# Later loads of x, early products of ones and a shifted zero fill in a chunked attention and mixture-of-experts kernel

## The chip, the cores and the metric

The kernel runs on one core of one Trainium2 chip. The metric is the device time of one execution in microseconds. "TensorE" (PE in the profile) multiplies matrices, "VectorE" (DVE) and "ScalarE" (ACT) work on elements, "GpSimd" (POOL) issues indirect transfers, and "SyncE" (SP) issues most of the other transfers.

## The reference

Chunked attention is followed by a mixture of experts, of which each token takes one. All is float32.

```python
B, H, S, D = 4, 8, 768, 64            # batch, heads, sequence, width of a head
chunk, left_ctx, right_ctx, n_mem = 32, 16, 8, 8
for c in range(S // chunk):
    k_full = concatenate([mem_k, k[l_start:r_end]])      # 8 memory keys + the chunk with its contexts
    v_full = concatenate([mem_v, v[l_start:r_end]])
    a = softmax(q_c @ k_full.T / sqrt(D))
    out[c] = a @ v_full

x = out.transpose(0, 2, 1, 3).reshape(3072, 512)         # token x (head, width)
logits = x @ w_gate                                      # 8 experts
e = argmax(logits); gate = softmax(logits)[e]
y = gate * (relu(x @ w1[e]) @ w2[e])                     # w1: 8 x 512 x 1024, w2: 8 x 1024 x 512
```

## The kernel before

**Attention.** The work is done in 32 steps of 96 queries (`QB`), step i of them in the loop `for i in range(NB)` (lines 1134 to 1176). Two steps share one load of queries and one load of keys (`load_q`, `load_k`, lines 626 to 636), "superblock" j. SyncE issues these loads, and the loads of v (`load_v`), in program order on its own queue. The buffers hold three superblocks of k and q and six steps of v. The tiles come with the tokens on the partitions, so TensorE turns them (transposes against an identity): `turn_q(m)` and `turn_k(m)` (lines 651 to 680) turn half of a superblock's heads, m = 2j or 2j + 1, into a PSUM bank, and ScalarE or VectorE copy the bank to SBUF. The bank is one of the two of the pool `ps_t`, or one that the caller hands over. `scores(i)` multiplies turned keys and queries (four products of 128 x 128 by 192 columns), and ScalarE takes three exponentials of the result. `values(i, g, bank)` multiplies by v one step later.

Ahead of the loop, superblocks 0 and 1 are turned: `turn_k(0)` and `turn_k(1)` into `ps_t`, `turn_q(0)` and `turn_q(1)` into two banks `first` of the pool `ps_o`, and `turn_k(2)` and `turn_k(3)` into the two halves of one tile `second` of the pool `ps_s`, which `scores` uses too (lines 1125 to 1132). In step i of the loop come, in this order, the loads for three steps ahead, `turn_q(i + 2)`, `scores(i)`, `values(i - 1)`, the turn of finished rows, and `turn_k(i + 4)`. The order of each engine's instructions is that of the program (`manual_schedule`); waits are put in by the framework where tiles depend on each other.

**Routing.** Eight groups of steps get logits, the choice of expert and a row number for each token. The work of a group is queued three steps after its last step and done piece by piece in later steps. Each token's row is then scattered to `x_dram`, a DRAM buffer sorted by expert, by indirect transfers of GpSimd (`scatter_one`, line 847). `behind(i)` (line 841) makes a transfer wait for the TensorE instruction that was issued last. Rows 0 to 255 of `x_dram` are filled with zeros ahead of that: two transfers on GpSimd's queue, written in step 2 (lines 1171 to 1173), which wait for nothing of that step. The rows behind each expert's tokens are filled later (`end_rows`).

**Experts.** From line 1244 on a planner writes the work: `op` (line 1278) notes each step with the semaphore counts it waits for, in program order for each engine, and `emit` writes it. For each expert TensorE has a switch over arms, one for each number of token columns (lines 1840 to 1848): "split" arms do each layer in seven products on sums of blocks (`layer`, line 1545), "plain" arms, for few tokens, do it directly (`plain`, line 1672). A hint for the next expert's arm is put three steps (plain: one) ahead of the arm's end. In a plain arm an engine has fewer steps than in a split one, so its last step raises its semaphore to the count of the split arm (`upto`). In this run experts 1 and 6 are plain. Between two arms `interlude(e)` (line 1639) turns the outputs of expert e - 1 (`turn_y`) and does first sums for expert e.

SyncE's queue in the expert part is what the change is about. In `expert(e)`:

- `load_x(e + 1)` (lines 1402 to 1416) brings the tokens of the next expert in eight transfers of 160 KB, into the one buffer `X`. VectorE empties `X` with two transposes, `turn_x(e + 1, 0)` and `turn_x(e + 1, 1)`, in the second layer of expert e (line 1793), and after them does two weight sums and one token sum `t1[0]` for expert e + 1.
- `get_w(e + 2, 0)` (line 1477) loads w1 of the expert after the next, 2 MB, once ScalarE has come to the middle of expert e.
- `get_w(e + 2, 1)` loads w2 of it, 2 MB, after ScalarE's last output of expert e.

Since the loads of x stand first in `expert(e)`, they come behind w2 of expert e + 1 on the queue, which was issued at the end of expert e - 1.

Of the kernel before, what the change touches and what calls it, by code (L numbers as in the profile page):

```python
# [12 lines left out]
I32 = mybir.dt.int32  # L13
# [13 lines left out]
N, DM, E, F = B * S, H * D, 8, 1024  # L27
# [44 lines left out]
NER = 256  # L72
TAIL = 192
# [454 lines left out]
def ordinary(ctx, tc, q, k, v, mem_k, mem_v, moe_w_gate, moe_w1, moe_w2, out, good):  # L528

    nc = tc.nc  # L530
# [12 lines left out]
    def bc(ap, axis, n):  # L543
        shape = list(ap.shape)
        shape.insert(axis, n)
        idx = tuple([slice(None)] * axis + [None])
        return ap[idx].to_broadcast(shape)
# [339 lines left out]
    def scatter_some(n):  # L887
        while spread and n:
            spread.pop(0)()
            n -= 1  # L890

    def need(i, f, *lists):
        if 0 <= i < NB:
            f(i)
# [219 lines left out]
    with tc.manual_schedule():  # L1114
        load_k(0)
        load_q(0)
        load_k(1)
        load_q(1)
        load_v(0)
        load_k(2)  # L1120
        load_v(1)
        load_q(2)
        load_v(2)

        first = [ps_o.tile([128, 512], F32, tag="o", name="o") for _ in range(2)]
        second = ps_s.tile([128, 2, 512], F32, tag="s", name="sc")
        turn_k(0)
        turn_k(1, nc.scalar.copy)
        turn_q(0, nc.vector.tensor_copy, first[0])
        turn_q(1, bank=first[1])  # L1130
        turn_k(2, bank=second[:, 0])
        turn_k(3, nc.scalar.copy, second[:, 1])
        early_rows()
        for i in range(NB):
            if i // 2 + 3 < NSB:
                (load_k, load_q)[i % 2](i // 2 + 3)
            need(i + 3, load_v)
            need(i + 2, turn_q)
            scores(i)
            scatter_some(1)  # L1140
            banks = [ps_o.tile([128, 512], F32, tag="o", name="o") for _ in range(2)]
            cur["bank"] = banks[0]
            if i <= 23:
                routing(1, "p")
            if i >= 1:
                values(i - 1, 0, banks[0])
            need(i - 2, turn_xb)
            routing(5 if i > 23 else 3)
            done = [g for g in range(len(GROUPS)) if i - 3 == GROUPS[g][1] - 1]
            late = logits(done[0], banks[1]) if done else None  # L1150
            if i >= 1:
                values(i - 1, 1, banks[1])
            if late:
                place_logits(*late)
            if i > 23:
                routing(1, "p")
            scatter_some(1)
            need(i + 4, turn_k)
            routing(6 if i > 23 else 5)
            hold_back()  # L1160
            for g in done:
                work.extend(routed(g))
            if i == 24:
                fetch_w(0, 4)
            if i >= 24:
                fetch_piece(1)
                fetch_piece(1)
            if len(scatters) >= EARLY and "early" not in cur:
                cur["early"] = i
                early_count(banks[0])  # L1170
            if i == 2:
                nc.gpsimd.dma_start(x_dram[0:TAIL].rearrange("(x p) c -> p x c", x=2), bc(zeros.bitcast(I32), 1, 2))
                nc.gpsimd.dma_start(x_dram[TAIL:NER], zeros[0 : NER - TAIL].bitcast(I32))
            if i == 29:
                early_load()
                early_gather()

        do_early(1)
        n = NB

        def bank_pair():
            banks = [ps_o.tile([128, 512], F32, tag="o", name="o") for _ in range(2)]
            cur["bank"] = banks[0]
            return banks

        banks = bank_pair()
        values(n - 1, 0, banks[0])
        scatter_some(1)  # L1190
        turn_xb(n - 2)
        late = last_logits(n - 3, banks[1])
        values(n - 1, 1, banks[1])
        scatter_some(1)
        nc.vector.tensor_copy(*late)
        routing(99, "v")
        fetch_w(1, 1)
        fetch_piece(4)
        do_early(1)
        banks = bank_pair()  # L1200
        late = last_logits(n - 2, banks[1])
        nc.vector.tensor_copy(*late)
        do_early(1)
        turn_xb(n - 1)
        scatter_some(1)
        do_early(1)
        routing(1, "p")
        routing(99, "v")
        hold_back()
        banks = bank_pair()  # L1210
        late = last_logits(n - 1, banks[1])
        nc.vector.tensor_copy(*late)
        fetch_piece(1)
        work.extend(routed(len(GROUPS) - 1))
        routing(99)
        check_sums()
        do_early(2)
        scatter_some(1)
        routing(1, "p")
        routing(99, "v")  # L1220
        hold_back()
        do_early(1)
        scatter_some(1)
        count_up()
        index = []

        def load_index(e):
            index.append(nc.tensor.value_load(cases[0:1, e : e + 1], min_val=0, max_val=len(arms_of(e)) - 1))

        while spread:  # L1230
            scatter_some(1)
            if len(early_ops) == 2:
                load_index(0)
            do_early(1)
        zeroed = end_rows(0)
        for j in scatters:
            tc.declare_no_dep(zeroed.ins, j, reason="rows behind those of the tokens")
        assert len(early_ops) == len(index) == 1
        rv = nc.values_load(good[0:1, 0:1], min_val=0, max_val=1)
        tc.switch_hint({mybir.EngineType.PE: index[0]}, len(arms_of(0)), "expert0")  # L1240
        nc.tensor.addr_align(PAGE, 0, 0)
        do_early(1)
# [514 lines left out]
    def expert(e):  # L1757
        A1, A2 = quarters(e, 0), quarters(e, 1)
        B1 = [[xT[:, 2 * k : 2 * k + 2, 1 - y] for y in range(2)] for k in range(2)]
        b1 = [[x_names(k, y) for y in range(2)] for k in range(2)]  # L1760
        B2 = [[h[:, 4 * k : 4 * k + 4, y] for y in range(2)] for k in range(2)]
        b2 = [[[("h", k, m, y) for m in range(2)] for y in range(2)] for k in range(2)]
        t1n, t2n = [("t1", i) for i in range(3)], [("t2", i % 2) for i in range(3)]
        s1n, s2n = [("s1", i) for i in range(3)], [("s2", i % 2) for i in range(3)]
        s2, (s1, t1) = sums2[e], sums1[e]
        t2 = token_sums(B2, b2, T2, "t2", t2n)
        w1n = [("w1", e % 2, "rest"), ("w1", e % 2, "21")]
        w2n = [("w2", e % 2, "rest"), ("w2", e % 2, "21")]
        if e + 1 < E:
            load_x(e + 1)  # L1770

        def usual():

            for a in range(2):
                hs = [[h[:, 4 * a + 2 * m : 4 * a + 2 * m + 2, y] for y in range(2)] for m in range(2)]
                hn = [[("h", a, m, y) for y in range(2)] for m in range(2)]
                part = [[A1[m][k][:, :, a] for k in range(2)] for m in range(2)]
                at = {
                    0: {5: [t1[2], s1[3]], 6: [t1[3]], 3: [s2[0]]},
                    1: {1: [t2[0]], 6: [s2[1]], 2: [s2[3]]},  # L1780
                }[a]
                layer(e, part, w1n, [x[:, :, a] for x in S1], s1n, B1, b1, T1, t1n, hs, hn, True, a == 1, at)
            assert not sends
            half.append(("ACT", counts["ACT"]))
            if e < E - 1:
                get_x(e + 1)
                tick()
            ys = [[yT[:, 2 * m : 2 * m + 2, 1 - y] for y in range(2)] for m in range(2)]
            yn = [[("y", m, y) for y in range(2)] for m in range(2)]
            at = {1: [t2[1]], 5: [t2[2], s2[2]], 6: [t2[3]]}  # L1790
            if e + 1 < E:
                s1e, t1e = sums1[e + 1]
                at[6].append(lambda: turn_x(e + 1, 0))
                at.update({2: [lambda: turn_x(e + 1, 1)], 7: [s1e[0]], 3: [s1e[1]], 4: [t1e[0]]})
            layer(e, A2, w2n, S2, s2n, B2, b2, T2, t2n, ys, yn, False, True, at)
            assert not sends

        half = []
        either(e, usual, (lambda ends: plain(e, ends)) if can_be_plain(e) else None)
        if e + 2 < E:  # L1800
            get_w(e + 2, 0, half)
        if 0 < e < E - 1:
            op("POOL", one_op(nc.gpsimd.drain))
        if e + 2 < E:
            get_w(e + 2, 1, [("ACT", counts["ACT"])])
# [113 lines left out]
```

## Time and profile before

| | us |
|---|---|
| median of three runs (490.04, 490.1, 492.1) | 490.1 |
| profiled execution | 488.05 |
| its span, first to last instruction | 486.2 |
| TensorE busy | 462.1 |
| VectorE busy | 282.5 |
| ScalarE busy | 207.8 |

A row of a timeline gives the start and the duration in us, the engine, the line, the operation, the tiles (out <- in), their shapes and the number of merged instructions; in brackets stands how long the engine was idle before, and what released it. "SPq" is SyncE's queue, at the time of issue; the transfer comes later. One float32 product shows as two MATMUL records. L534 and L539 are the helpers through which all products and turns go, so the tiles tell them apart: `tqk`, `kn` and `qn` are turns of keys and queries, `sc` scores, `sum_p` to `sum_z` the banks of the experts, `xs` the buffer `X`, `xsT` its transposed form, `yT` the outputs ahead of their turn, and `t` and `s` sums of tokens and weights. DMA queues: q1 is SyncE's, q0 GpSimd's, q8 the one that brings code.

### The profile page before, as it was taken

The page shows a single profiled execution, that of the slowest core. Times are in us where ns is not written, and L with a number is a line of the kernel's source. Part 1 is how long each engine was busy: PE and PEld are TensorE (multiplying, and loading weights), DVE is VectorE, ACT ScalarE, POOL GpSimd, SP SyncE. Part 2 cuts the span into 40 slices and gives each one's busy share as a digit, 9 for nine tenths or more (in the row PEclk, how much of TensorE's full clock was granted, in tenths as well). Part 3 has the DMA queues.
Part 4 walks back from the last instruction along what each step waited for, and adds up shares of the span by engine and source line. Part 5 has one row for each costly group of instructions (what it writes and reads, how often), then busy time and mean ns, then how long its engine had stood idle before and what let it go on. Part 6 is the DMA issues. An engine that isn't in the chain of part 4 may idle for free. (4 is left out here: it accounts for less than half of the span.)

```text
span 486.2 us, 9257 instructions
## 1 busy us (share of the span) xinstructions
PE 462.1 (95%) x3272; PEld 431.4 (89%) x3272; DVE 282.5 (58%) x548; ACT 207.8 (43%) x389; POOL 146.1 (30%) x191
## 2 busy tenths in 40 slices
PE   4999999999999899999999999999999999899992
PEld 3899999999998679899999999977778999889992
DVE  4466676677555668924665867644537784555511
ACT  3676666666632236311452353334214623144312
POOL 3000323323353227334054144022311442442004
PEclk9999999999999999999999999999999999999998
DMA  9999999999989588790997386390714787400002
GB/s 235 176 196 203 207 265 240 239 227 251 283 191 303 154 248 192 158 295 20 222 275 166 102 253 144 67 283 34 152 25 140 241 176 217 124 3 27 1 1 89
DMA packets 103058, 82.98 MB, mean 171 GB/s; under 512 B 40309, under 2 KB 85966, under 8 KB 102992
## 3 DMA queue, kind: packets, MB, share of 16 engines
q1 hardware_dynamic: 94576, 67.94, 59.6%
q0 software_dynamic: 6912, 13.54, 8.4%
q8 instruction: 44, 0.72, 0.7%
q10 hardware_dynamic: 1504, 0.59, 0.5%
q14 instruction: 22, 0.18, 0.1%
HBM read 65.62 MB, written 21.28 MB: 179 GB/s over the span
## 5 line engine op out<-in xcount | busy, mean ns | idle before, releaser
L1446 POOL DMA_INDIRECT out_dram<-y,lab x42 | 50.3, 1198 | 149.0 <-ACT y L1433 30.8
L935 POOL DMA_INDIRECT lab<-x_dram,rows x42 | 51.3, 1222 | 53.9 <-PE sum_q L534 19.6
L534 PE MATMUL o<-v,ex 128*96 128x65 f32 x512 | 52.8, 246 | 0.0
L534 PEld LDWEIGHTS o<-v,ex 128*96 128x96 f32 x512 | 50.4, 165 | 1.4 <-issue 1.3
L534 PE MATMUL sum_p<-xsT,w 128*128 128x144 f32 (+7 forms) x256 | 49.1, 337 | 2.7 <-DVE t L1379 1.7
L534 PE MATMUL sc<-qT,kT 128*128 128x192 f32 x256 | 49.2, 336 | 0.0
L534 PEld LDWEIGHTS sum_p<-xsT,w 128*128 128x128 f32 x256 | 41.8, 190 | 7.0 <-issue 2.6
L534 PE MATMUL sum_p<-h,w 128*128 128x144 f32 (+7 forms) x256 | 46.1, 335 | 0.0
L848 POOL DMA_INDIRECT x_dram<-xr,dest x32 | 29.7, 928 | 52.3 <-PE o L534 34.0
L705 ACT ACTIVATE ex<-sc,cst 128x256 f32<-128x256 f32 x96 | 38.6, 472 | 14.2 <-PE sc L534 12.0
L534 PEld LDWEIGHTS sum_p<-h,w 128*128 128x128 f32 x256 | 41.8, 190 | 2.4
L534 PEld LDWEIGHTS sc<-qT,kT 128*128 128x128 f32 x256 | 42.0, 195 | 0.0
L656 ACT COPY qT<-tqk 64x384 f32<-64x384 f32 x60 | 30.0, 500 | 28.0 <-PE tqk L539 27.2
L1382 ACT COPY sum_r<-sum_p 128x640 f32<-128x640 f32 x36 | 24.4, 677 | 40.9 <-PE sum_p L534 40.6
L674 DVE COPY kT<-tqk 64x384 f32<-64x384 f32 x58 | 32.0, 552 | 11.0 <-PE tqk L539 10.5
L534 PE MATMUL sum_r<-t,w 128*128 128x144 f32 (+5 forms) x192 | 37.0, 340 | 0.0
L534 PE MATMUL sum_p<-t,s 128*128 128x144 f32 (+5 forms) x192 | 36.8, 340 | 0.0
L534 PE MATMUL sum_q<-t,s 128*128 128x144 f32 (+5 forms) x192 | 36.7, 339 | 0.0
L1400 DVE STREAM_TRANSPOSE xsT<-xs 128x1280 f32<-128x1280 f32 (+1 forms) x16 | 22.4, 1426 | 23.9 <-DMA xs<-x_dram 23.9
L534 PEld LDWEIGHTS sum_q<-t,s 128*128 128x128 f32 x192 | 31.9, 190 | 2.3
L534 PEld LDWEIGHTS sum_p<-t,s 128*128 128x128 f32 x192 | 31.9, 190 | 2.4
L534 PEld LDWEIGHTS sum_r<-t,w 128*128 128x128 f32 x192 | 31.8, 190 | 2.3
(183 smaller groups left out, 771.0 us busy)
## 6 DMA issues: line engine op xcount, KB each, us to landing
w<-in_moe_w_dram SPq DMA_DIRECT2D x36, 512.0 KB
w<-in_moe_w_dram SPq DMA_DIRECT2D x7, 2048.0 KB
xs<-x_dram SPq DMA_DIRECT2D x56, 160.0 KB
kn<-in_k_dram SPq DMA_DIRECT2D x16, 384.0 KB
qn<-in_q_dram SPq DMA_DIRECT2D x16, 384.0 KB
x_dram<-zeros SPq DMA_DIRECT2D x8, 396.0 KB
v<-in_v_dram SPq DMA_DIRECT2D x24, 128.0 KB
v<-in_v_dram SPq DMA_DIRECT2D x24, 112.0 KB
```

The lines of the kernel that those rows point to most:

```text
L534: i = nc.tensor.matmul(*args, **more)
L656: copy(to[:, :, :, t], tq[D * t : D * t + D])
L674: i = copy(to, of[:, :, 0:PAIRS].rearrange("d a (y z p) -> d a y z p", y=2, z=2))
L705: nc.scalar.activation(ex4[:, :, :, sl], sc4[:, :, :, sl], AF.Exp, bias=mask[:, 3 * x + g : 3 * x + g + 1], scale=D**-0.5)
L848: i = nc.gpsimd.indirect_dma_start(out=x_dram, out_offset=bass.IndirectOffsetOnAxis(ap=dest[:, t : t + 1], axis=0), in_=xr[:, t % NXR].bit ...
L935: return nc.gpsimd.indirect_dma_start(out=to.bitcast(I32), out_offset=None, in_=x_dram.rearrange("r (k c) -> (r k) c", c=LB), in_offset=ba ...
L1382: op("ACT", one_op(lambda: nc.scalar.copy(to, of)), reads, writes)
L1400: op("DVE", one_op(lambda: nc.vector.transpose(to, of)), [("xs", y, a) for a in range(4)], [("x", k, 1 - y) for k in range(2)])
L1446: return nc.gpsimd.indirect_dma_start(out=out, out_offset=bass.IndirectOffsetOnAxis(ap=which.bitcast(I32), axis=0), in_=y, in_offset=None, ...
```

## The change

There are four edits.

1. Ten products of a 128 x 128 tile of ones with itself, into a bank that is overwritten later, stand ahead of TensorE's first turn.
2. `turn_k(2)` goes to a bank of `ps_t`, and `turn_k(3)` to the first half of `second`: two tiles instead of one. In step 0, `turn_q(2)` stands behind `scores(0)` instead of ahead of it.
3. The zero fill of rows 0 to 255 moves from step 2 to the end of step 5 (the sixth), and waits for TensorE's last instruction there.
4. `load_x(e + 1)` at the start of expert e stays for e = 0 alone. For the others, `load_x(e + 2)` stands in expert e between the loads of w1 and w2 of expert e + 2. It waits for the two transposes that empty `X`.

```diff
         first = [ps_o.tile([128, 512], F32, tag="o", name="o") for _ in range(2)]
         second = ps_s.tile([128, 2, 512], F32, tag="s", name="sc")
+        for _ in range(10):
+            mm(first[0][:, 0:128], lhsT=ones, rhs=ones, start=True, stop=True)
         turn_k(0)
         turn_k(1, nc.scalar.copy)
         turn_q(0, nc.vector.tensor_copy, first[0])
         turn_q(1, bank=first[1])
-        turn_k(2, bank=second[:, 0])
-        turn_k(3, nc.scalar.copy, second[:, 1])
+        turn_k(2)
+        turn_k(3, nc.scalar.copy, second[:, 0])
         early_rows()
         for i in range(NB):
...
             need(i + 3, load_v)
-            need(i + 2, turn_q)
+            if i > 0:
+                need(i + 2, turn_q)
             scores(i)
+            if i == 0:
+                need(i + 2, turn_q)
...
-            if i == 2:
-                nc.gpsimd.dma_start(x_dram[0:TAIL].rearrange("(x p) c -> p x c", x=2), bc(zeros.bitcast(I32), 1, 2))
-                nc.gpsimd.dma_start(x_dram[TAIL:NER], zeros[0 : NER - TAIL].bitcast(I32))
+            if i == 5:
+                behind(
+                    nc.gpsimd.dma_start(
+                        x_dram[0:TAIL].rearrange("(x p) c -> p x c", x=2), bc(zeros.bitcast(I32), 1, 2)
+                    )
+                )
+                behind(nc.gpsimd.dma_start(x_dram[TAIL:NER], zeros[0 : NER - TAIL].bitcast(I32)))
...
-        if e + 1 < E:
-            load_x(e + 1)
+        if e == 0:
+            load_x(1)
...
         either(e, usual, (lambda ends: plain(e, ends)) if can_be_plain(e) else None)
         if e + 2 < E:
             get_w(e + 2, 0, half)
+            load_x(e + 2)
         if 0 < e < E - 1:
             op("POOL", one_op(nc.gpsimd.drain))
```

## The prediction

> **What bounds the kernel now.** First the page: engines, slices, DMA rate.
>
> ```profile
> span 486.2 us, 9257 instructions
> ...
> PE 462.1 (95%) x3272; PEld 431.4 (89%) x3272; DVE 282.5 (58%) x548; ACT 207.8 (43%) x389; POOL 146.1 (30%) x191
> ...
> DMA packets 103058, 82.98 MB, mean 171 GB/s; under 512 B 40309, under 2 KB 85966, under 8 KB 102992
> ```
>
> TensorE is busy for 462.1 of 486.2 us, so a change that adds no speed to its products can win only some of the 24 us that are left. Second, who those 24 us wait for: the waits with TensorE as filter.
>
> ```profile
> PE tqk L539 <- DMA kn<-in_mem_k_dram: 6.0, 1, 6.0
> PE sum_z L539 <- DVE t L1379: 2.0, 1, 2.0
> PE sum_p L534 <- DVE t L1379: 1.7, 1, 1.7
> PE sc L539 <- DVE kT L674: 1.2, 1, 1.2
> PE tqk L539 <- DMA kn<-in_k_dram: 0.7, 2, 0.4
> ```
>
> Three belong to the start (tqk, sc), two to the experts (sum_z, sum_p). Third, the stretches of the start: after TensorE's count come DVE, ACT and POOL, then granted clock, share of the DMA engines and GB/s.
>
> ```profile
> 0.00:15.00 15.00, 7.75 (x36) 6.83 (x36) 5.44 (x12) 5.58 (x11) 4.56 (x21) 1.00 0.99 223
> 15.00:30.00 15.00, 14.34 (x137) 14.15 (x138) 8.48 (x22) 10.64 (x25) 0.00 (x0) 1.00 1.07 181
> 30.00:60.00 30.00, 30.00 (x308) 29.56 (x307) 20.51 (x65) 19.78 (x47) 3.10 (x8) 1.00 1.10 202
> ```
>
> The DMA engines are full (shares about 1) through the first 60 us. TensorE waits for loads until about 23 us, and from 30 us on for nothing: two bounds lie close together. Fourth, the timeline of the start.
>
> ```profile
> 0.84 0.17 DVE L583 MEMSET ones<- 128x128 f32 x1 [0.84 <-PEq L1905]
> ...
> 6.04 1.57 PE L539 MATMUL tqk<-cst,kn 100*128 100x100 f32 x8 [6.04 <-DMA kn<-in_mem_k_dram]
> ...
> 10.84 0.90 PE L539 MATMUL sc<-cst,kn 96*128 96x96 f32 x4 [1.22 <-DVE kT L674]
> ...
> 12.18 2.82 PE L534 MATMUL sc<-qT,kT 128*128 128x192 f32 x8
> ...
> 12.79 1.00 ACT L656 COPY qT<-tqk 64x384 f32<-64x384 f32 x2
> ...
> 15.03 1.21 ACT L705 ACTIVATE ex<-sc,cst 128x256 f32<-128x256 f32 x3 [1.24 <-PE sc L534]
> ...
> 15.24 0.58 PE L539 MATMUL tqk<-cst,kn 96*128 96x96 f32 x4 [0.25 <-DMA kn<-in_k_dram]
> ...
> 15.99 1.49 PE L534 MATMUL sc<-qT,kT 128*128 128x192 f32 x8
> ...
> 23.02 0.52 PE L539 MATMUL tqk<-cst,kn 96*128 96x96 f32 x4 [0.41 <-DMA kn<-in_k_dram]
> ```
>
> The scores of step 0 take 2.82 us, those of step 1, the same eight records, 1.49: TensorE runs at half rate until about 15 us, though the windows print 1.00 there.
>
> **The change, part by part: the start.** *Ten products.* At half rate a record of 192 columns takes 2.82 / 8 = 0.35 us, so one of 128 columns some 0.235, and ten products of two records 4.7 us (an estimate from that row). They need only the ones, ready at 1.01, so they end near 5.7, ahead of the 6.04 at which the first keys land: cost 0, at most 0.3 us if TensorE starts late. What they can bring is the full rate for what follows.
>
> ```profile
> L539 PE MATMUL tqk<-cst,kn x120: 246/246/401, 6.0 to 123.5; 96*128 96x96 f32 x88, 100*128 100x100 f32 x32
> ...
> L539 PE MATMUL sc<-cst,kn x8: 364/367/420, 8.8 to 11.4; 96*128 96x96 f32 x8
> ```
>
> (min/median/max ns.) A turn took 367 ns at 8.8 to 11.4 us and 246 later; the rate rose only after the unbroken stretch from 10.84 to 15.0, 4.2 us. I take it that 4.7 us of products do the same. [...]
>
> *Banks and order.* The fourth key turn no longer waits 1.22 us for DVE to empty the tile it shared with the third; `turn_q(2)` goes behind the scores of step 0, so its ACT copies (1.00) go behind that step's exponentials (1.21). TensorE then comes to the next key turn, `turn_k(4)`, near 13.8 at half rate (15.0 less 1.2) and some 2 us sooner at full rate. But that turn already waits 0.25 us for its keys, which land at 15.24. What is late next is this load, so all three edits together are worth what the load gives, and no more. At half rate the later ACT copy would hold `turn_q(3)` up and take back up to 1.0.
>
> *Zero fill.* It is issued at 3.57 us now, beside the first loads. The DMA queues from 6.9 to 10.6 us (packets, MB, share of 16 engines):
>
> ```profile
> q1 hardware_dynamic: 1793, 0.73, 76.4%
> q0 software_dynamic: 160, 0.54, 37.7%
> ```
>
> The fill (0.54 MB) takes 37.7% of 3.7 us, 1.4 us of all 16 engines. With the engines full, every load behind it lands 1.4 us sooner: `turn_k(4)` at 13.8, and the keys of 23.02, for which TensorE waits again, at 21.6. Bounds: by bytes, 0.54 MB at the 181 GB/s of the second stretch, 3.0 us; or nothing, since the load queue moved 0.73 MB in those 3.7 us, 197 GB/s, no slower than alone. I take 1.4, the fill's own row. At step 5 the fill waits for TensorE's last turn there, about 34 us; GpSimd has nothing else until the first group's routing, which is queued in step 7. Its 1.4 us are then paid by loads that are fetched some two steps ahead, in a stretch where TensorE is busy 30.00 of 30: cost 0, up to the whole 1.4 if that lead is used up.
>
> **The experts.** Loads of x for expert e+2 now go between w1 and w2 of that expert, one expert sooner. Where this pays is the end of expert 6, a plain one:
>
> ```profile
> 388.82 1.75 SPq L1484 DMA_DIRECT2D w<-in_moe_w_dram  x4
> ...
> 404.44 11.24 SPq L1411 DMA_DIRECT2D xs<-x_dram  x8
> ```
>
> ```profile
> 394.18 2.90 DVE L1400 STREAM_TRANSPOSE xsT<-xs 128x1280 f32<-128x1280 f32 x2
> ...
> 414.29 4.72 PE L534 MATMUL sum_q<-h,w 128*128 128x168 f32 x32
> ...
> 418.63 1.51 DVE L1400 STREAM_TRANSPOSE xsT<-xs 128x1280 f32<-128x1280 f32 x1 [11.54 <-DMA xs<-x_dram]
> 418.85 4.72 PE L534 MATMUL sum_p<-h,w 128*128 128x168 f32 x32
> ...
> 420.81 1.51 DVE L1400 STREAM_TRANSPOSE xsT<-xs 128x1280 f32<-128x1280 f32 x1 [0.67 <-DMA xs<-x_dram]
> ...
> 424.60 0.87 DVE L1379 TENSOR_TENSOR t<-xsT 128x640 f32<-128x640 f32 x1
> 425.53 0.65 PE L539 MATMUL sum_z<-cst,yT 128*128 128x128 f32 x4 [1.96 <-DVE t L1379]
> ...
> 428.00 1.93 PE L534 MATMUL sum_p<-xsT,w 128*128 128x248 f32 x8
> ```
>
> DVE waits 11.54 us for expert 7's x, then does two transposes, two weight sums and t, and TensorE's turn of the outputs starts when t is done (425.47): in a plain arm t carries DVE's count up to the end that the turn waits for. After the change x can be issued when its buffer is free, 397.1 (394.18 + 2.90), behind w1 of 388.82. At the mean 171 GB/s, 2.1 MB of w1 (12.3 us) and 1.3 MB of x (eight loads of 160 KB, 7.7 us) end near 409. The next late thing is the second transpose, which overwrites what the first layer reads until 414.29; then 1.51 and the 3.15 us from 422.32 to 425.47 give 419.0, and TensorE wants its turn at 423.57 (418.85 + 4.72). So this wait goes, with 4.6 us to spare. From turn to next product the plain expert 1, without such a wait, takes 2.95 us:
>
> ```profile
> 229.16 0.60 PE L539 MATMUL sum_z<-cst,yT 128*128 128x128 f32 x4
> ...
> 232.11 1.17 PE L534 MATMUL sum_p<-xsT,w 128*128 128x216 f32 x5 [0.34 <-issue]
> ```
>
> 423.57 + 2.95 = 426.5 against 428.00: 1.5 us won, 2.0 if the 2.47 of expert 6 holds. Elsewhere x came before TensorE needed it: nothing is won. The new wait on SP (for the transposes of x) has w2 behind it; w2 waits for ACT's last output anyway, and is needed only in the expert after the next, so cost 0.
>
> **Sum.** 1.4 + 1.5 = 2.9 us. The profiled execution took 488.05 us, its span and 1.85 around it: 485.15. The median of the runs is 490.1, 2.05 above the profiled one, so I forecast 490.1 - 2.9 = 487.2. The measurement tells some 0.5%, 2.45 us.
>
> **The rivals.** *Start gives nothing.* The fill's DMA time is only moved, from one full stretch (0.99, 1.07) into another (1.10), and loads after step 6 are late by what was won; or the rate stays at half and the ACT order takes it back. Against it: no wait of TensorE in 30 to 60 us. Then only 1.5 is left: 488.6. [...] Chance 0.22.
>
> *More.* The fill costs by bytes, 3.0, and the turn 2.0: 485.1. Chance 0.14.
>
> *Slower: TensorE's code comes late.* TensorE reads its arm's code by DMA. Before expert 1 it was idle 1.73 us; the row names t, but at expert 6 the same product started before its t. Rows of the DMA queues at 196 to 202.5 and at 202.5 to 206 us:
>
> ```profile
> q1 hardware_dynamic: 356, 1.30, 99.1%
> ```
>
> ```profile
> q1 hardware_dynamic: 48, 0.08, 13.8%
> q8 instruction: 2, 0.03, 8.5%
> ```
>
> ```profile
> 207.43 2.95 PE L534 MATMUL sum_p<-xsT,w 128*128 128x200 f32 x16 [1.73 <-DVE t L1379]
> ```
>
> The code moved only once w1 had drained. Now x stands right behind w1 on that queue, 1.3 MB or 7.7 us at 171 GB/s. If code waits for x as well, it comes at 210 (202.5 + 7.7) instead of by 206, and TensorE waits some 4 us more there, and as long at expert 6, where w1 (388.82 + 12.3) drains shortly ahead of the arm too. It decides once x's transfer runs past the start of the arm. Against it: in the code the hint that asks for the next arm stands ahead of the last three products, at about the place where x is released, so x need not be ahead of it in the queue. 487.2 + 2 x 4 = 495. Chance 0.10.
>
> **How the numbers follow.** The forecast has 0.54, and its own range is 485.5 to 489 (start 0.4 to 2.4, turn 1.5 to 2.0). Range for all: 484.9 to 490.4; it leaves out the slower rival and the tails. Faster by over 0.5% (below 487.65): the forecast's larger part and all of "more", 0.55. Within: the rest of the forecast and the first rival, 0.35. Slower 0.10.
>
> **What would show it.** Right: the turn of 15.24 near 13.8 and that of 23.02 near 21.6, each still waiting for keys; the scores of step 0 near 1.5 us; no transpose waiting for xs in experts 1 and 6; expert 6's turn without a wait, its next product 2.9 us sooner. Wrong: a wait for kn, qn or v between 30 and 50 us, or a longer wait than 1.73 ahead of expert 1, or a new one ahead of the others.

## The result and the profile after

| | before | after |
|---|---|---|
| median of five runs each, us | 491.1 (490.04 to 493.06) | 497.53 (497.05 to 498.57) |
| profiled execution, us | 488.05 | 497.1 |
| its span, us | 486.2 | 495.3 |

The ratio is 1.0128, with a 95% interval of 1.0099 to 1.0157: the change costs 6.4 us. The forecast was 487.2, the range 484.9 to 490.4, from the 490.1 of three runs; the result lies outside it, on the side that had a chance of 0.10.

The page of after, with the granted clock in 40 slices of 12.4 us, and the waits of TensorE (total, times, longest):

```profile
span 495.3 us, 9295 instructions
...
PE 468.6 (95%) x3292; PEld 438.5 (89%) x3292; DVE 281.9 (57%) x548; ACT 207.4 (42%) x389; POOL 145.8 (29%) x191
...
PEclk9899999999999899989999999999999998999997
```

```profile
PE sum_p L534 <- DVE s L1388: 5.4, 2, 3.0
PE tqk L539 <- DMA kn<-in_k_dram: 3.8, 2, 3.1
PE sum_r L534 <- issue: 3.3, 1, 3.3
```

TensorE is busy 6.5 us longer than the 462.1 of before, of which the ten products are 4.05; and 5.4 us in two waits are put to `sum_p`, the first product of an expert. The clock row says how the two hang together: besides the last slice, four slices are at 8, the second, fourteenth, eighteenth and thirty-fourth, and in each lies one of the waits of 3.1, 3.3, 3.0 and 2.4 us or what follows it. The timeline of TensorE shows the four places:

```profile
1.06 4.05 PE L534 MATMUL o<-ones 128*128 128x128 f32 x20 [1.06 <-DVE ones L583]
...
9.66 1.49 PE L534 MATMUL sc<-qT,kT 128*128 128x192 f32 x8
...
14.56 0.85 PE L539 MATMUL tqk<-cst,kn 96*128 96x96 f32 x4 [3.08 <-DMA kn<-in_k_dram]
...
15.84 2.56 PE L534 MATMUL sc<-qT,kT 128*128 128x192 f32 x8
...
167.54 0.45 PE L534 MATMUL sum_r<-nought 128*128 128x320 bf16 x2 [3.29 <-issue]
167.82 10.46 PE L534 MATMUL sum_z<-w,h 128*128 128x128 f32 x32
...
211.78 4.62 PE L534 MATMUL sum_p<-xsT,w 128*128 128x200 f32 x16 [2.98 <-DVE s L1388]
...
413.49 4.20 PE L534 MATMUL sum_p<-xsT,w 128*128 128x168 f32 x16 [2.38 <-DVE s L1388]
417.52 2.44 PE L534 MATMUL sum_q<-xsT,w 128*128 128x168 f32 x16
...
433.48 0.60 PE L539 MATMUL sum_z<-cst,yT 128*128 128x128 f32 x4
...
436.22 1.93 PE L534 MATMUL sum_p<-xsT,w 128*128 128x248 f32 x8 [0.40 <-issue]
```

Read each bracket together with the duration behind it. The scores of step 0 are at full rate now (1.49 us for eight records), those of step 1, behind a wait of 3.08 us, are not (2.56). The first products of experts 1 and 6 take 4.62 and 4.20 us, where the same groups took 2.95 and 2.52 before: 1.7 us more each, behind waits that were 1.73 and 0.30 us and are 2.98 and 2.38 now. The turn at the end of expert 6 (433.48) waits for nothing; before it waited 1.96. The rows of before at the entry of the expert part and at expert 6, besides 207.43 and 425.53 shown with the prediction:

```profile
166.09 0.45 PE L534 MATMUL sum_r<-nought 128*128 128x320 bf16 x2 [2.06 <-issue]
166.37 8.82 PE L534 MATMUL sum_z<-w,h 128*128 128x128 f32 x32
...
405.09 2.52 PE L534 MATMUL sum_p<-xsT,w 128*128 128x168 f32 x16 [0.30 <-issue]
```

Lining up the starts of the same groups in both traces gives the account. The shift is what after is late by at that point:

| TensorE's group | before | after | shift |
|---|---|---|---|
| turn of keys ahead of step 1 | 15.24 | 14.56 | -0.68 |
| two turns later | 23.02 | 23.21 | +0.19 |
| entry of the expert part (`sum_r`) | 166.09 | 167.54 | +1.45 |
| first product of expert 0 | 175.02 | 178.12 | +3.10 |
| first product of expert 1 | 207.43 | 211.78 | +4.35 |
| second group of expert 1 | 210.21 | 216.25 | +6.04 |
| first product of expert 6 | 405.09 | 413.49 | +8.40 |
| second group of expert 6 | 407.45 | 417.52 | +10.07 |
| turn at the end of expert 6 | 425.53 | 433.48 | +7.95 |
| last turn | 477.28 | 485.50 | +8.22 |

Three parts stand out. The start gained 0.68 us and lost it again. At expert 1, wait and half rate cost 1.25 + 1.69 = 2.9 us; at expert 6, 2.1 + 1.67 = 3.8, of which the turn without its wait gives 2.1 back. The remaining 2.9 us between 23 and 178 us (3.10 - 0.19) lie at the entry of the expert part, which the change does not touch: its wait was 2.06 us in the profiled run of before and 3.29 here, and the group behind it ran at half rate (10.46 us where it was 8.82). This part differs between profiles without a change to it: in the twelve kernels below, all with the same code there and one profile each, the wait was 1.89 to 3.52 us, and the group behind it took 8.82 us in four and 9.91 to 11.33 in eight. The profiled run of before had it short and at full rate, and was 488.05 where its median is 491.1. What the change itself cost is thus about 8.2 - 2.9 = 5.3 us up to the last turn. The span has 0.9 us more behind that turn (9.8 us where before has 8.9); this stretch takes 8.9 to 10.4 us in the fourteen profiled kernels, so nothing shows that the change made it longer. The medians say 6.4 us, with 4.9 to 7.7 by the interval.

### The profile page after: what moved, and what is told of

Its sections match the earlier page's. It is cut to its first block, busy times and chain, and to the rows that moved or that the text cites. A ratio compares the mean times of both kernels' runs of the same rounds, so it can differ in the third digit from the quotient of the medians.

```text
span 495.3 us, 9295 instructions
## 1 busy us (share of the span) xinstructions
PE 468.6 (95%) x3292; PEld 438.5 (89%) x3292; DVE 281.9 (57%) x548; ACT 207.4 (42%) x389; POOL 145.8 (29%) x191
## 5 line engine op out<-in xcount | busy, mean ns | idle before, releaser
L534 PE MATMUL sum_p<-xsT,w 128*128 128x144 f32 (+7 forms) x256 | 52.5, 354 | 6.7 <-DVE s L1388 5.4
L534 PEld LDWEIGHTS sum_p<-xsT,w 128*128 128x128 f32 x256 | 45.1, 203 | 10.9 <-issue 8.5
L674 DVE COPY kT<-tqk 64x384 f32<-64x384 f32 x60 | 33.1, 552 | 9.8 <-PE tqk L539 9.2
```

Of the source, the lines that this page charges most:

```text
L534: i = nc.tensor.matmul(*args, **more)
L674: i = copy(to, of[:, :, 0:PAIRS].rearrange("d a (y z p) -> d a y z p", y=2, z=2))
```

## The experiments

The times of before beside them were 490.19, 490.79, 491.04 and 491.03 us in four sessions; each ratio is against the runs of its own session, and comes from all of them, so it is not quite the quotient of the medians.

**Two halves.** `start_only` has edits 1 to 3 and the loads of x of before; `x_only` has edit 4 alone.

> Only the edits of the start (ten products, banks and order, zero fill); the loads of x stand as before. Theory code (the time is lost at experts 1 and 6, where x right behind w1 holds back the read of the next arm's code, TensorE idles over 2 us and then runs at half rate for 3.4 us): within 1.5 us of before, 490 to 492; TensorE's wait ahead of expert 1 at most 2 us and of expert 6 at most 0.5, the 2 us stall at the end of expert 6 back. Rival start (the 3.1 us wait for keys at step 0 and the half rate behind it cost the time): 3 us or more above before, 494 or more.

> Only the loads of x between w1 and w2; the start as before. Theory code: 3.5 to 6 us above before, 494 to 497; waits of 2 to 4 us ahead of experts 1 and 6, each followed by products at half rate, no stall at the end of expert 6. Rival start: about 2 us below before, 489.

Measured: start_only 491.8 us, ratio 1.0026 (0.9999 to 1.0053); x_only 495.98, ratio 1.0124 (1.0088 to 1.016). The moved loads alone lose nearly all of it, as theory "code" said, and the start gains nothing (its interval is 0 to 2.6 us lost). In start_only the waits ahead of experts 1 and 6 are 0.93 and 0.30 us, and the stall at the end of expert 6 is back, with 1.15 us of the 2 that were expected. In x_only expert 1 starts late by nearly the same amounts as in after, with the starts of TensorE's groups:

```profile
211.60 4.62 PE L534 MATMUL sum_p<-xsT,w 128*128 128x200 f32 x16 [2.98 <-DVE s L1379]
...
412.98 4.19 PE L534 MATMUL sum_p<-xsT,w 128*128 128x168 f32 x16 [2.26 <-issue]
```

The first bracket names a weight sum of VectorE, the second nothing. The products of these arms use no such sum, and in hint_one_sooner below the product of expert 1 starts at 205.56 while this sum ends at 207.19; the name is only what happened to end last. A sounder candidate is the queue that brings code, q8. (Another queue, q14, brings code too, in reads of half the size: in before 22 of them moved 0.18 MB, and 44 of q8 0.72; that q8's are TensorE's is taken from the starts that follow them.) Two windows of 0.2 and 0.1 us in x_only, 205.2 to 205.4 and 208.3 to 208.4, hold one read each (share of 16 engines: 41.0% of 0.2 us x 16 is a read of 1.3 us, 79.2% of 0.1 us x 16 another); between the two none begins:

```profile
q8 instruction: 1, 0.02, 41.0%
...
q8 instruction: 1, 0.02, 79.2%
```

The second read ends near 209.6, and the product starts at 211.60, about 2.0 later. In before, both reads of this place begin between 202.5 and 202.8 us, and the product starts at 207.43:

```profile
q8 instruction: 2, 0.03, 99.6%
```

The loads of x explain the gap in time: SyncE issues them from 201.58 on in after, ahead of both reads.

```profile
201.58 6.66 SPq L1420 DMA_DIRECT2D xs<-x_dram  x8
208.33 0.78 SPq L1492 DMA_DIRECT2D w<-in_moe_w_dram  x1
```

**x behind the arm's end.** x still goes ahead of w2, but waits for ScalarE's last output of the arm, as w2 does.

```diff
             get_w(e + 2, 0, half)
-            load_x(e + 2)
...
         if e + 2 < E:
+            load_x(e + 2, [("ACT", counts["ACT"])])
             get_w(e + 2, 1, [("ACT", counts["ACT"])])
```

> As x_only, but x of expert e+2 also waits for ScalarE's last output of expert e, so it stands just ahead of w2 on the queue and is not in flight while the next arm's code is read. Theory code: waits ahead of expert 1 at most 2 us and of expert 6 at most 0.5, no half rate, no stall at the end of expert 6 (x has still the whole plain arm): 1 to 2.5 us below before, 488 to 490. Rival (x ahead of w2 is what costs, for example through w2's later landing): as x_only, 494 to 497.

Measured: 489.41 us, ratio 0.9992 (0.9963 to 1.0021). The loss is gone, though the gain of 1 to 2.5 us on before does not show. SyncE's row is the first below, TensorE's are the second fence:

```profile
207.52 5.69 SPq L1411 DMA_DIRECT2D xs<-x_dram  x8
```

```profile
209.65 2.94 PE L534 MATMUL sum_p<-xsT,w 128*128 128x200 f32 x16 [1.24 <-DVE t L1379]
...
407.31 2.52 PE L534 MATMUL sum_p<-xsT,w 128*128 128x168 f32 x16 [0.30 <-issue]
...
425.62 0.60 PE L539 MATMUL sum_z<-cst,yT 128*128 128x128 f32 x4
```

Issued six us later, x holds nothing up: both first groups are at full rate, and the turn at expert 6's end still does not wait. From the first product of expert 1 to expert 7's this kernel takes 218.6 us (209.65 to 428.26), before 220.6 (207.43 to 428.00): in these two traces the 2 us of the stall are won. The times do not show them: by the interval of the ratio this kernel wins 1.8 us at most.

**The hint earlier.** If the code comes late, an earlier hint might mend it: x_only with the hint seven steps ahead of the arm's end instead of three.

```diff
-                    if i == len(arm) - (1 if kind == "plain" else 3) and e + 1 < E:
+                    if i == len(arm) - (1 if kind == "plain" else 7) and e + 1 < E:
```

> As x_only, but the hint for the next arm stands ahead of the second layer in split arms (seven products ahead of the arm's end instead of three), so that code is asked for before x is released. Theory code, if it is the hinted page that comes late: the waits ahead of experts 1 and 6 fall to under 1 us, no half rate there, and the time is 4 us or more below x_only, near 489. If it is another page (the one behind the arm): as x_only within 1 us. Rival (x's landing or another wait, not code): as x_only within 1 us.

Measured: 517.43 us, ratio 1.0576 (1.0538 to 1.0614). Neither expectation held. The timeline of TensorE shows why:

```profile
203.19 2.12 PE L534 MATMUL sum_r<-t,w 128*128 128x144 f32 x16
210.49 1.02 PE L539 MATMUL sum_z<-cst,yT 128*128 128x128 f32 x4 [5.18 <-issue]
...
217.10 4.63 PE L534 MATMUL sum_p<-xsT,w 128*128 128x200 f32 x16 [2.54 <-DVE s L1379]
```

TensorE now stands 5.18 us inside expert 0's arm, ahead of its last turns, and 2.54 us again at the start of the next. One code read begins at 207.6 and ends at 208.9, 1.6 us ahead of the first restart; the next begins between 214.3 and 214.4 and ends near 215.3, 1.8 us ahead of the second. My reading is that the hinted code took the place of code that the arm had still to run, so that it had to be read again, and the hinted code after it. The same happens at the ends of expert 3 (2.52 and 4.11 us) and 5 (4.57 and 1.39). That a wait of TensorE follows a read is shown; what code is kept at hand is inferred from it.

**What holds the read: bytes or pieces?** Two kernels add to x_behind_arm a load of no use right behind w1, where x stood. `extra_long` loads as many bytes as x, 1.31 MB, in 256 long pieces; `extra_short` loads as many pieces, 2560, with an eighth of the bytes.

```diff
             get_w(e + 2, 0, half)
+            extra(e + 2)
...
+    def extra(e):
+        def fn(n):
+            made = []
+            for k in range(8):
+                to = X[32 * (k % 4) : 32 * (k % 4) + 32, k // 4]
+                of = moe_w2[e].rearrange("f d -> (f d)")[32 * 128 * NBL * k : 32 * 128 * NBL * (k + 1)]
+                made.append(nc.sync.dma_start(to.rearrange("p b f -> p (b f)"), of.rearrange("(p f) -> p f", p=32)))
+            return made
+        op("SP", fn, [], [("xs", y, a) for y in range(2) for a in range(4)], dma="extra", by=128)
```

In extra_short the source is `x_dram[0 : 32 * NBL, 0:16]`, row by row.

> The kernel x_behind_arm (489.4 us; waits at the starts of experts 1 and 6: 1.24 and 0.30 us) with one thing more: right behind w1 of expert e+2, SP also loads 1.31 MB of weight rows into the buffer xs, in long pieces (5 KB per partition, 256 in all, where x has 2560 of 512 B); the real x overwrites it behind the arm. Nothing that the kernel computes uses the added bytes. It repeats the early transfer in bytes and place, but not in its number of pieces. Theory 'bytes' (TensorE's second code read waits behind the bytes that are queued on the DMA engines): the second read comes 3 to 4 us behind the first as in x_only, the waits ahead of experts 1 and 6 are 2.3 to 3.0 us, their first products run at half rate, 493 to 497 us. Theory 'pieces' (what holds it is the many short pieces of x, or SP working them out): the second read comes 0.3 to 1.5 us behind the first, waits as in x_behind_arm, 488 to 491 us.

> The kernel x_behind_arm with one thing more: right behind w1 of expert e+2, SP also loads 2560 pieces of 64 B (0.16 MB, as many pieces as x has, an eighth of its bytes) from the first rows of x_dram into the buffer xs; the real x overwrites them behind the arm. Nothing that the kernel computes uses them. Theory 'pieces': the second code read comes 3 to 4 us behind the first, waits of 2.3 to 3.0 us ahead of experts 1 and 6, 493 to 497 us. Theory 'bytes': 0.16 MB hold it by a few tenths of a us at most, waits as in x_behind_arm (1.24 and 0.30 us), 488 to 491 us.

Measured: extra_long 499.2 us, ratio 1.0188 (1.0132 to 1.0244); extra_short 490.48, ratio 0.9998 (0.997 to 1.0026). SyncE was as long at issuing the short pieces (6.76 us from 204.33) as it is for x. So neither the pieces nor their issue holds the read; the bytes do: extra_short's two reads begin within 0.2 us, extra_long's 2.6 us apart. But extra_long came out above its expected 493 to 497 us. TensorE in it:

```profile
209.32 4.63 PE L534 MATMUL sum_p<-xsT,w 128*128 128x200 f32 x16 [2.68 <-DVE s L1379]
...
282.09 1.56 PE L534 MATMUL sum_p<-xsT,w 128*128 128x192 f32 x8 [2.94 <-issue]
...
413.70 4.20 PE L534 MATMUL sum_p<-xsT,w 128*128 128x168 f32 x16 [2.29 <-DVE s L1379]
```

It took longer than after because a third start is late (282.09, expert 3). As I read it, the real x and w2 come later, and so the next weights and their added load fall on the end of expert 2 too: in the three stretches of 4 us from 270 us on, SyncE's transfers took 99%, 102% and 68% of the DMA engines' time, in x_only 85%, 69% and 21%.

**How many bytes.** `extra_quarter` is extra_long with two of its eight loads, 0.33 MB.

```diff
-            for k in range(8):
+            for k in range(2):
...
-        op("SP", fn, [], [("xs", y, a) for y in range(2) for a in range(4)], dma="extra", by=128)
+        op("SP", fn, [], [("xs", y, a) for y in range(2) for a in range(4)], dma="extra", by=32)
```

> The kernel extra_long (499.2 us) with two of its eight added loads: 0.33 MB of long pieces right behind w1, where extra_long adds 1.31 MB. Nothing that the kernel computes uses the added bytes. Theory 'bytes' (the code read waits its turn behind what is queued ahead of it; 1.31 MB at 0.2 to 0.3 MB per us are 4 to 6 us, of which about 3 us lie behind the moment of the read): 0.33 MB are through by 1 to 1.5 us behind w1's end, the second read comes 0.3 to 1.5 us behind the first, the waits ahead of experts 1 and 6 are under 2 us and the clock stays, 488 to 491 us. Rival 'any transfer there': the reads are held as in extra_long, waits of 2.3 us or more, 494 us or more.

Measured: 489.67 us, ratio 0.9996 (0.9969 to 1.0023); theory "bytes" holds, with a gap of 1.6 us where 1.5 at most was expected. Put in order, with the start of the second read taken from windows of 0.1 to 0.3 us of the DMA queues (before and x_behind_arm: both reads in one window):

| kernel | bytes behind w1 | first read, us | second read | second behind first | wait ahead of expert 1 | its first group |
|---|---|---|---|---|---|---|
| x_behind_arm | 0 | 204.8 to 205.4 | same window | under 0.6 | 1.24 | 2.94 |
| extra_short | 0.16 MB | 207.6 to 207.8 | same window | under 0.2 | 1.84 | 2.94 |
| extra_quarter | 0.33 MB | 205.8 to 206.0 | 207.4 to 207.6 | 1.6 | 1.64 | 2.94 |
| extra_long | 1.31 MB | 203.4 to 203.6 | 206.0 to 206.2 | 2.6 | 2.68 | 4.63 |
| x_only | 1.31 MB | 205.2 to 205.4 | 208.3 to 208.4 | 3.0 | 2.98 | 4.62 |
| after | 1.31 MB | 205.0 to 205.2 | 208.6 to 208.8 | 3.6 | 2.98 | 4.62 |

The waits ahead of expert 6 are 0.30, 0.30, 0.30, 2.29, 2.26 and 2.38 us in the same order. The gap of extra_long is shorter than the 3 to 4 us that theory "bytes" gave it. In all six the product comes 1.7 to 2.2 us behind the end of the second read. Without bytes behind w1 the wait is still 1.2 to 1.8 us (before: 1.73), because both reads begin only 3 to 3.6 us ahead of the arm's end.

Each read brings 0.02 MB (the rows of q8). The gap went neither with the number nor with the length of the pieces: it was 3.0 us with x, 2560 pieces of 512 B, and 2.6 with extra_long, 256 pieces ten times as long, for the same 1.31 MB.

**The hint one step sooner.** x_behind_arm with the hint four steps ahead instead of three.

> The kernel x_behind_arm (489.4 us, waits ahead of experts 1 and 6 of 1.24 and 0.30 us) with the hint to the next arm four steps ahead of an arm's end and not three. Theory 'late read': the hint's read comes a step (0.7 to 1.5 us) sooner and lands sooner, the wait ahead of expert 1 falls to 0.5 us or less, and nothing else changes; 488 to 489.5 us. Theory 'displaced' (what x_only_hint_early shows: the hinted code takes the place of code that the arm has still to run): new waits of 1 us or more inside the arms or at their starts, 491 us or more.

Measured: 488.86 us, ratio 0.9967 (0.9938 to 0.9996). Theory "late read" holds, but for 0.06 us of wait more than expected:

```profile
205.56 2.94 PE L534 MATMUL sum_p<-xsT,w 128*128 128x200 f32 x16 [0.56 <-DVE y L1435]
```

The wait fell from 1.24 to 0.56 us, and no new one came inside the arms. The two reads now begin near 199.8 and 201.4 us, 5.2 and 3.6 ahead of the arm's end, and the second ends 2.7 us ahead of the product, so it is not what the last 0.56 us wait for. Four steps are early enough for the read and late enough for the arm. Seven were not, though they were tried with x behind w1.

**The start: the zero fill alone.** `zero_only` is before with edit 3 alone.

> The kernel before with the zero fill moved to step 6 and nothing else. Between 7 and 15 us the profiled run of before moved 4150 pieces and 1.56 MB on SP's queue beside 0.54 MB of zeros, start_only 4313 pieces and 1.63 MB without zeros, after 4396 and 1.64. Theory 'pieces' (SP's loads are held by their many short pieces, and the zeros' bytes ran beside them): SP's queue moves 4250 to 4450 pieces in that window, the keys of block 4 come 0.3 to 0.5 us sooner, and TensorE, which is busy until 15.0 us, gains no more than its wait of 0.25 to 0.65 us; the time is that of before within 1 us. The prediction's own term: the whole 1.4 us, with more than 4700 pieces in the window, and a turn of keys at 23.0 us that comes 1 us or more sooner.

Measured: 491.16 us, ratio 1.0008 (0.9978 to 1.0039). SyncE's queue between 7 and 15 us (packets, MB, share), in zero_only:

```profile
q1 hardware_dynamic: 4239, 1.60, 125.5%
```

This queue moved 3701 to 4150 pieces in that window in the eight profiled kernels that have the fill there (before the most), and 4239 to 4518 in the six that don't. The means, 3878 and 4331, differ by 453 pieces, 0.8 us at 541 pieces per us; zero_only alone is just under its expected 4250. So the loads seem to get back 0.8 us of the fill's 1.4, an estimate from these counts; five of the six kernels have the other edits of the start too, and zero_only by itself is 361 pieces or 0.7 us above the mean of the eight. TensorE did not get even these: the turn of before's 23.02 us came at 22.98.

**The start: the wait filled.** `start_fill` is start_only with twelve more products of ones in the wait for keys of step 0.

```diff
             cur["bank"] = banks[0]
+            if i == 0:
+                for _ in range(12):
+                    mm(banks[1][:, 0:128], lhsT=ones, rhs=ones, start=True, stop=True)
```

> Edits at the start alone (as start_only, 491.8 us), and twelve more products of ones between the queries of step 1 and the keys of block 4, where start_only's TensorE stood 3.5 us for a load and then ran its second step at half rate (scores 2.6 us where 1.5 us is the full rate). Theory 'clock' (the wait itself costs nothing, the half rate behind it cancels the start's gain): the wait shrinks to about 1 us, the second step runs at the full rate, the fourth turn of keys (at 23.0 us before) comes 0.8 to 1.5 us sooner than in start_only and before, and the time is 0.8 to 1.5 us less than start_only's, 490 to 491 us. Rival 'loads': keys and values come no sooner than before, so that the step after waits for them as long as the clock saves; 491 to 492.5 us.

Measured: 491.6 us, ratio 1.001 (0.9982 to 1.0038). The time sided with the rival, the trace with neither fully:

```profile
9.92 2.81 PE L534 MATMUL sc<-qT,kT 128*128 128x192 f32 x8
12.52 0.85 PE L539 MATMUL tqk<-cst,qn 96*128 96x96 f32 x4
13.16 2.96 PE L534 MATMUL o<-ones 128*128 128x128 f32 x24
15.95 0.49 PE L539 MATMUL tqk<-cst,kn 96*128 96x96 f32 x4
16.28 0.49 PE L539 MATMUL tqk<-cst,qn 96*128 96x96 f32 x4
16.61 1.49 PE L534 MATMUL sc<-qT,kT 128*128 128x192 f32 x8
```

Step 1 is at full rate, as theory "clock" said. But this time step 0 was at half rate in spite of the ten products, and the filler ended after the keys had come, so the turn came at 15.95, later than start_only's 15.26.

**Together.** `both` is start_fill with x behind the arm; `all_mends` is both with the hint four steps ahead and eight filling products.

> start_fill together with x behind the arm's last output (x_behind_arm, 489.4 us beside 490.2 before). If the two gains are separate: the stall at expert 6's end gone (2.0 us), the wait ahead of expert 1 at or under 1.7 us, the start 1 us sooner; 487 to 489 us, 1.5 to 3 us below before. If the start's gain does not reach the end: 489 to 490.5 us.

> The kernel both (489.6 us, 0.9965 of before) with the hint four steps ahead of an arm's end, and eight products of ones in the wait of step 0 in place of twelve, which there ended after the keys had come. If the parts add up: the wait ahead of expert 1 about 0.6 us (1.5 in both), the stall at expert 6's end gone, the second step of the start at the full rate behind a wait under 1 us; 487 to 489 us, a ratio of 0.992 to 0.996. If the start gives nothing, as in the runs so far: the time of hint_one_sooner, a ratio of 0.996 to 0.998.

Measured: both 489.59 us, ratio 0.9965 (0.9934 to 0.9997); all_mends 487.48, ratio 0.9944 (0.9913 to 0.9975). In `both` the start's gain does not reach the end: step 0 ran at half rate, the filler ended late again (the turn came at 16.89), and the wait ahead of expert 1 was 1.51 us. all_mends is inside what its parts should add up to. It is the shortest of all kernels here, 0.6% below before, where the change as it was made is 1.3% above. Its timeline:

```profile
10.93 1.98 PE L534 MATMUL o<-ones 128*128 128x128 f32 x16
13.72 0.52 PE L539 MATMUL tqk<-cst,kn 96*128 96x96 f32 x4 [0.82 <-DMA kn<-in_k_dram]
14.08 0.49 PE L539 MATMUL tqk<-cst,qn 96*128 96x96 f32 x4
14.41 1.49 PE L534 MATMUL sc<-qT,kT 128*128 128x192 f32 x8
...
21.75 0.52 PE L539 MATMUL tqk<-cst,kn 96*128 96x96 f32 x4 [0.87 <-DMA kn<-in_k_dram]
...
205.22 2.94 PE L534 MATMUL sum_p<-xsT,w 128*128 128x200 f32 x16 [0.56 <-DVE y L1447]
```

Here the filler keeps the wait at 0.82 us, the clock holds, and the turns stand at 13.72 and 21.75, the 13.8 and 21.6 of the prediction. One kernel is no proof that the start is worth 1.3 us: beside hint_one_sooner, which has the start of before and ran in another session, the medians differ by 1.4 us, and the intervals of the ratios overlap.

## Why the prediction was wrong

**The step that failed** is the last of "The experts": "The new wait on SP (for the transposes of x) has w2 behind it; w2 waits for ACT's last output anyway, and is needed only in the expert after the next, so cost 0." It asked what stands behind x on SyncE's own queue. It should have asked what else the DMA engines have to move in those 8 us, and the answer was the code of the next arm. The measured price is 2.9 us at expert 1 and 3.8 at expert 6.

**The rival that was right** is "TensorE's code comes late", at the places it named. Its own count of 4 us each was near, but differently made: the read comes 3 us later and not 7.7, the waits grow by 1.25 and 2.1 us, and half rate behind them adds 1.7 each, a term it did not have. Its chance of 0.10 rested on "x need not be ahead of it in the queue", since the hint stands ahead of the last three products "at about the place where x is released". The place in the program is not the order in time: x is issued from 201.58 us on, as VectorE empties the buffer, and the first code read begins at 205.0 to 205.2. The prediction had the time of that release for expert 7 (397.1); the trace of before has the arm's end there at 404.8, some 8 us later, and the two were not compared.

**Expert 6's end.** The forecast was 1.5 to 2.0 us. The turn lost its wait as told, in after, x_only and x_behind_arm; the shift falls by 2.12 us from 10.07 to 7.95, and by 1.85 up to the next product (428.00 before, 436.22 after). Right, but outweighed.

**The start.** The forecast was 1.4 us, from the zero fill's 37.7% of 3.7 us. The fill's absence is worth some 0.8 us to the loads, by the counts above. The ten products took 4.05 us where 4.7 was estimated, and held nothing up. TensorE got 0.68 us sooner to its keys, then ran step 1 at half rate, 1.1 us longer, because it had waited 3.08 us. The prediction took "what the load gives, and no more" as the worth of edits 1 and 2, and gave the waiting no price but its length. In spite of the ten products, the clock through the first two steps differs between profiles: step 0 was at full rate in after and start_only, at half in start_fill; step 1 the other way about. The old start does the same: of the eight kernels that have it, step 1 took 1.49 us in five (before among them) and 2.02 to 2.82 in three, and the turn of before's 23.02 came between 22.47 and 24.96. So one trace beside another cannot price this part. The interval of start_only says 0 to 2.6 us lost; for this part the first rival, "start gives nothing", holds.

**Fill at step 6.** Cost 0 as told: no wait for loads shows between 30 and 60 us in after.

**What stays open.** Why a read on a queue of its own waits for bytes of another queue. The windows show that it does (2.6 to 3.6 us behind 1.31 MB), and the pieces and their issue are ruled out; whether the request itself leaves later, no row tells. Whether the new start, with the wait filled, is worth anything is open as well. Whether hinted code takes the place of other code, and of which, was not tried beyond the three places of the hint.

## What to carry to other kernels

Before moving a large load, lay its transfer beside every other queue's rows in that stretch, the code queue's above all when a switch or a jump lies ahead; 1.3 MB in the wrong 8 us cost three times what they won, and 6 us later they cost nothing. A wait of TensorE had two prices here, its length and the half rate that followed many waits of 2.1 to 3.5 us (some 1.7 us each), so a saving that only moves a wait to a place where it is longer can be a loss. Put the hint for the next code as early as the current code allows, one step at a time: four steps took 0.68 us off a wait, seven cost 21 us (with x behind w1, beside x_only).

## What the runs showed of the hardware

- **TensorE fell to half rate behind a wait of 2.10 us, and not behind each longer one.** At the entry of the expert part the same code makes the test by itself. In `both` a wait of 2.10 us is followed by half rate, in x_only one of 3.12 is not:

```profile
167.01 0.45 PE L534 MATMUL sum_r<-nought 128*128 128x320 bf16 x2 [2.10 <-issue]
167.30 10.47 PE L534 MATMUL sum_z<-w,h 128*128 128x128 f32 x32
```

```profile
168.99 0.45 PE L534 MATMUL sum_r<-nought 128*128 128x320 bf16 x2 [3.12 <-issue]
169.28 8.82 PE L534 MATMUL sum_z<-w,h 128*128 128x128 f32 x32
```

  At the starts of experts, half rate followed waits of 2.26 to 2.98 us but not one of 2.94 (extra_long, expert 3). It cost about 1.7 us in most cases (4.62 for 2.95, 4.20 for 2.52, 10.47 for 8.82), and 2.5 at the entry of start_only (11.33). The windows of after show it while it lasts; the third field from the end is the granted clock, and eight records fit into 2 us at 0.51, fourteen at 1.00:

```profile
212.00:214.00 2.00, 2.00 (x9) 2.00 (x9) 0.46 (x1) 0.00 (x0) 0.00 (x0) 0.64 1.06 282
214.00:216.00 2.00, 2.00 (x8) 2.00 (x7) 0.00 (x0) 0.00 (x0) 0.00 (x0) 0.51 1.06 411
216.00:218.00 2.00, 2.00 (x14) 2.00 (x13) 0.00 (x0) 0.57 (x1) 0.70 (x1) 1.00 0.75 287
```

  In after, ahead of the last turn, the granted clock is 0.50 in four stretches of 3.41 us, from 14.59, 168.19, 212.56 and 413.95 us, and 1.00 outside them from 4.35 on, where its records begin. The four starts lie 3, 48, 61 and 120 times 3.413 us behind 4.35. In the 3.41 us ahead of each, TensorE was busy for 0.34 to 1.04 us, so idle for 2.4 to 3.1; of the other such steps the least busy, the one from 4.35 on, has 1.98 us busy. In before the clock is 1.00 from 15.39, where the records begin, to 483.01, behind the last turn; counted from 15.39, the wait of 2.06 us at the entry falls on two steps, which are busy for 1.87 and 2.89 us (162.16 to 165.57 and on to 168.98).

  My reading is that it goes by where the wait falls. In x_only the clock is 0.79 from 211 to 212 us, which puts the start of half rate at 211.58; thirteen steps earlier, 167.2 lies inside the wait of 3.12 us and divides it into 1.4 and 1.8. In extra_long it is 0.72 from 209 to 210, so half rate starts at 209.44; 21 steps later, 281.1 divides the 2.94 into 2.0 and 1.0. These places are estimates from those windows and the steps of after.
- **The second code read came later behind more bytes of another queue.** With 1.31 MB queued behind w1 the second read began 2.6 to 3.6 us behind the first, with 0.33 MB 1.6 us, with 0.16 MB in 2560 pieces within 0.2.
- **A hint can cost.** Four steps ahead brought the wait ahead of expert 1 to 0.56 us; seven steps ahead made TensorE stand 5.18 us inside the arm that was still running.
